# Attention with feature maps and two wide layers on one core: grouping the small matmuls and re-planning the order

## The chip, the cores and the metric

One core of a Trainium2 chip. The metric is the device time of one execution in microseconds (us). PE is the matmul engine, DVE the vector engine, ACT the scalar engine, POOL the general engine, SP the queue that issues the DMAs.

## What is computed

```python
def phi(x):                                   # x: 4 batches, 8 heads, 576 tokens, 64
    proj = np.einsum('bhsd,df->bhsf', x, w_phi)                   # 128 features
    proj = proj - np.max(np.abs(proj), axis=-1, keepdims=True)
    return np.concatenate([np.exp(proj), np.exp(-proj)], axis=-1)
q_p, k_p = (phi(q), phi(k))
kv = np.einsum('bhsf,bhsd->bhfd', k_p, v)
z = np.sum(k_p, axis=2)
num = np.einsum('bhsf,bhfd->bhsd', q_p, kv)
den = np.einsum('bhsf,bhf->bhs', q_p, z)[..., None] + 1e-06
x = num / den                                 # as 2304 tokens x 512
h = x @ w_in;  x = elu(h) @ w_out             # 512 -> 2048 -> 512
h = x @ w_in2; x = (h * cos(h)) @ w_out2      # 512 -> 2048 -> 512
```

## The kernel before, in words

The wide layers run as three passes of fp32r matmuls, high and low halves of both operands (`PASSES`). Layer 1 goes in two parts: the first 8 of 16 slices of d_ff over nine blocks of 256 tokens (part 0), then the other 8 over six blocks of 384 (part 1); layer 2 takes all 16 slices over six blocks of 384. For one block and one slice, `step` issues a group of 12 matmuls g1 (L636, into bank h), then the activation on ACT and DVE (L655, L658, L661 in layer 1; L670 to L682 in layer 2), the split into halves (L242 or L240 high, L694 low), and a group of 12 matmuls g2 (L644, into banks y). A block's own operand is split the same way (high half by ACT or DVE, low half by DVE, L595). Weights arrive packed; each of 128 pieces costs `convert_piece` and `split` three ACT instructions (L327, L330, L353), two on DVE (L334, L338) and two on POOL (L342, L356).

The attention is laid between the groups of part 0. `keys` takes the five key tiles of a batch: eight projections (L373), maximum and subtraction on DVE for each half of the heads ("odd" 0 and 1; L386, L389), two exponentials each on ACT (L423, L426), then the products with v (`times_v`, L431; for batch 0 also a sum over the tokens, L437). For the other batches the sum over the key tiles is made by additions of 1024 columns (L451), on POOL or DVE. `sums` turns the result (L488). `queries` and `results` do a tile of 128 queries: projections (L373), maximum and subtraction, four turns per half (L517), two exponentials per half (L520), 24 small matmuls per half (`product`, L535; 48 records where a matmul takes two), then L543, L546, L549 for the division, which writes the tile's part of the block's operand xy.

The order on every engine is made ahead of time. `body` lists tasks with an engine (or a choice of engines), a cost, a due time and what they wait for, and `plan` places them one by one: on the engine that can start first it takes, of the tasks that are ready, the one with the earliest due time. The due times come from the constants `BEGIN`, `BLOCK_A`, `LEAD`, `PACE` and so on. Until bank y1 is in use, `keep_busy` fills planned idle time of PE with matmuls on zeros ("spare", L749).

Of the kernel before, what the change touches and what calls it, by code (L numbers as in the profile page):

```python
# [13 lines left out]
ALU = mybir.AluOpType  # L14
# [34 lines left out]
SLACK = 1.0  # L49
# [36 lines left out]
class Task:  # L86


    def __init__(self, engine, cost, due, fn, writes=(), reads=(), after=(), latency=None, port=False):
# [3 lines left out]
        self.start = self.end = self.opens = None  # L93

# [27 lines left out]
def plan(tasks, opened):  # L122
# [29 lines left out]
    order, pooled = [], (0.0, 0.0)  # L152
    while len(order) < len(tasks):
        best = None
        for e, q in queues.items():
            cand = []
            for t in q:
                pl = place(t)
                if pl is not None:
                    slack = SLACK if t.engine == "SP" and pl[0] else 0.0  # L160
                    cand.append((max(t.ready, pl[0] + slack), t, pl[1]))
            if cand:
                first = max(free[e], min(c[0] for c in cand))
                c = min((c for c in cand if c[0] <= first), key=lambda c: c[1].due)
                if best is None or (first, c[1].choice[e]) < best[:2]:
                    best = (first, c[1].choice[e], e, c[1], c[2])
# [7 lines left out]
        for b, p in got:  # L174
            b.place = p
            held[p] = b
        t.start, t.end, t.cost = start, start + spent, spent
        if engine == "POOL":
            pooled = t.start, t.end
# [21 lines left out]
def mr_cost(n):  # L201

    return n * PE_COL + 0.013


def body(tc, qt, kt, vt, wphi, w1, w2, out):
# [54 lines left out]
    def buf(pool, tag, n, shape, dtype=F32):  # L261
        return Buf([(pool, f"{tag}{i}") for i in range(n)], shape, dtype)
# [102 lines left out]
    def shifted(x, due, r, ds, after, banks):  # L365
# [12 lines left out]
        task("PE", 1.04, due, project, pp, [x, c_w, *ds], after)  # L378
# [18 lines left out]
    def keys(b, due, pace, after=()):  # L397
# [4 lines left out]
        for t in range(5):  # L402
# [12 lines left out]
            if b == 0:  # L415
                shifted(kf, du - KFIRST, r, ds, (), ("a0", "a1", "h0", "h1"))
            else:
                shifted(kf, du, r, ds, (), AP)
            for odd in range(2):
                d, kv, e = ds[odd], kvs[odd], buf("at", "ek", NE, [P, 4, 2, NF])  # L420
# [7 lines left out]
                def times_v(kv=kv, e=e, v=v, t=t, r=r, odd=odd):  # L428
                    for i in range(4):
                        at, pair = 64 * (i % 2), i // 2  # L430
                        nc.tensor.matmul(  # L431
                            kv.tile[at:at + 64, pair * 256:pair * 256 + 256],
                            v.tile[0:r, 2 * i + odd], e.tile[0:r, i].rearrange("p s f -> p (s f)"),
                            start=(t == 0 and pair == 0), stop=(t == 4), skip_group_check=True,
                        )
                    for i in range(4 if zp else 0):
                        nc.tensor.matmul(  # L437
                            zp.tile[32 * i:32 * i + 32, 256 * odd:256 * odd + 256],
                            ones[0:r], e.tile[0:r, i].rearrange("p s f -> p (s f)"),
                            start=(t == 0 and odd == 0), stop=(t == 4), skip_group_check=True,  # L440
                        )

                a1 = task("ACT", cost(ACT_, 512), du, exp, [e], [d], d.ready)
                a2 = task("ACT", cost(ACT_, 512), du, exp_neg, [], [d, e], d.ready)
                if zp:
                    task("PE", 1.62, du, times_v, [kv, zp], [e, v], [a1, a2])
                    continue
                task("PE", 1.06, du, times_v, [kv], [e, v], [a1, a2])
                if t:
# [3 lines left out]
                    task("POOL", sums_of(1024), du, add, [totals[odd]], [e], [a1, a2])  # L453
# [42 lines left out]
    def queries(T, due, pace):  # L496
# [12 lines left out]
        for odd in range(2):  # L509
            results(T, odd, due + odd * pace / 2, parts, ds[odd], done)  # L510

    def results(T, odd, due, parts, d, done):
        e, m, tt, n = buf("at", "eq", NEQ, [P, 2, 4, P]), buf("at", "rd", 2, [P, P]), bank(*AQ), bank(*AQ)

        def turn():
            for h in range(4):
                nc.tensor.transpose(tt.tile[:, h * P:(h + 1) * P], d.tile[:, h], ident)  # L517

        def exp(neg):
            nc.scalar.activation(  # L520
                e.tile[:, neg], tt.tile.rearrange("p (h t) -> p h t", h=4), AF.Exp, scale=1.0 - 2 * neg
            )

        task("PE", 0.55, due, turn, [tt], [d, c_id], d.ready)
        a1 = task("ACT", cost(ACT_, 512), due, lambda: exp(0), [e], [tt])
        a2 = task("ACT", cost(ACT_, 512), due, lambda: exp(1), [], [tt, e])

        def product():
            for i, g in enumerate((2, 0, 1)):
                for b, lo, hi in parts:  # L530
                    k = kvz[b, odd].tile
                    for half in range(2):
                        for h in range(4):
                            at = 64 * (h % 2) + 32 * g
                            nc.tensor.matmul(  # L535
                                n.tile[32 * h:32 * h + 32, g * P + lo:g * P + hi],
                                k[:, half, h // 2, at:at + 32] if g < 2 else k[:, half, 2, 32 * h:32 * h + 32],
                                e.tile[:, half, h, lo:hi],
                                start=(i == 0 and half == 0 and lo == 0), stop=(half == 1), skip_group_check=True,
                            )  # L540

        def denominator():
            nc.scalar.activation(m.tile, n.tile[:, 2 * P:3 * P], AF.Identity, bias=eps)  # L543

        def inverse():
            nc.vector.reciprocal(m.tile, m.tile)  # L546

        def finish():
            nc.vector.tensor_tensor(  # L549
                out=xy[:, 2 * odd:2 * odd + 2, T * P:(T + 1) * P],  # L550
                in0=n.tile[:, 0:2 * P].rearrange("p (g t) -> p g t", g=2),
                in1=m.tile[:, None, :].to_broadcast([P, 2, P]), op=ALU.mult,
            )

        kz = [kvz[b, odd] for b, _, _ in parts]
        task("PE", 1.43 if len(parts) == 1 else 1.9, due, product, [n], [e, *kz], [a1, a2, *done])
        task("ACT", cost(ACT_, P), due, denominator, [m], [n])
        task("DVE", cost(RECIP, P), due, inverse, [m])
        xt[T] = xt.get(T, []) + [task("DVE", cost(DVE_, 256), due, finish, cells((2 * odd, 2 * odd + 1), T * P, P), [n, m])]


# [64 lines left out]
    def step(m, j, i, last, xs, ys, yp, hs, N, due, pace, late):  # L626
# [24 lines left out]
        in_line("g1", task("PE", 12 * mr_cost(N) + 0.05, d1, g1, [hp], [*wi, *x], line["g1"]))  # L651
# [161 lines left out]
```

## Time and profile before

| | us |
|---|---|
| three runs | 1006.4, 1008.87, 1006.4 (median 1006.4) |
| the profiled execution: span from first to last instruction | 1004.8 |
| PE busy in it | 986.5 (98%) |
| DVE, ACT, POOL busy | 730.0, 496.3, 241.9 |

The page gives no time for the profiled execution other than its span; the median of the runs is 1.6 us above it. Busy time of PE counts the spare matmuls. The times of instructions below are from the span's start.

### The profile page before, as it was taken

Reading aid. Unit: us, or ns where it says so; the run is one execution under the profiler, and the core shown is the slowest. Engines: PE = TensorE matmul, PEld = TensorE weight load, DVE = VectorE, ACT = ScalarE, POOL = GpSimd, SP = SyncE. Lnnn points to the kernel's source line nnn. Section 1 sums busy time; section 2 is a strip of 40 time slices with the busy share of each in tenths; the row PEclk is TensorE's granted clock in tenths of the full one; section 3 lists DMA queues with packets and bytes.
Section 4 is the critical chain, followed back from the end, with each engine's and each line's share of the span. In section 5 each row is a group of like instructions: output and inputs, shape, how many; then the busy total and the mean of one; then the engine's idle time right before and its main releaser. Section 6 shows DMA issues by size and latency. Waiting matters only on the chain.

```text
span 1004.8 us, 21194 instructions
## 1 busy us (share of the span) xinstructions
PE 986.5 (98%) x8404; PEld 943.2 (94%) x8404; DVE 730.0 (73%) x1434; ACT 496.3 (49%) x1192; POOL 241.9 (24%) x274
## 2 busy tenths in 40 slices
PE   9999999999999999999999999999999999999998
PEld 6797888998899999999999999999999999999998
DVE  6999788768677986997354699966666666666664
ACT  6987445545545875775232577532332232323322
POOL 2675303103101772774000276400000000000000
PEclk9999999999999999999999999999999999999999
DMA  6463031022102432441012143000000000000000
GB/s 197 163 201 102 7 107 54 30 78 59 39 13 96 151 124 87 160 158 36 8 32 74 64 137 113 29 33 1 1 32 1 1 33 1 33 1 1 32 1 32
DMA packets 46563, 63.30 MB, mean 63 GB/s; under 512 B 6400, under 2 KB 25472, under 8 KB 46464
## 3 DMA queue, kind: packets, MB, share of 16 engines
q1 hardware_dynamic: 46304, 61.88, 18.7%
q8 instruction: 66, 1.08, 0.5%
q14 instruction: 33, 0.27, 0.1%
q10 hardware_dynamic: 160, 0.07, 0.0%
HBM read 52.49 MB, written 9.44 MB: 62 GB/s over the span
## 4 chain that ended last, share of the span: by engine, by line
PE 81%; DVE 8%; POOL 3%; ACT 3%; issue 3%; DMA 1%; DVEq 0%; POOLq 0%; ACTq 0%
PE h L636 21%; PE y L644 20%; PE a L644 13%; PE a L636 13%; PE a L431 4%; PE a L535 4%; PE a L373 3%; POOL l L342 2%; DVE l L338 2%; POOL l L356 2%; PE a L517 1%; DVE l L334 1%; DVE u L694 1%; DVE u L595 1%; ACT l L327 1%
## 5 line engine op out<-in xcount | busy, mean ns | idle before, releaser
L636 PE MATMUL h<-u,h 128*128 128x256 f32 (+1 forms) x1152 | 254.6, 311 | 3.4 <-DVE u L661 3.4
L644 PE MATMUL y<-u,h 128*128 128x256 f32 (+1 forms) x1152 | 254.3, 311 | 1.0 <-DVE u L694 1.0
L636 PEld LDWEIGHTS h<-u,h 128*128 128x128 f32 x1152 | 191.9, 188 | 9.5 <-DVE u L661 4.2
L644 PEld LDWEIGHTS y<-u,h 128*128 128x128 f32 x1152 | 192.3, 188 | 4.6 <-issue 2.3
L644 PE MATMUL y<-u,l 128*128 128x256 f32 (+1 forms) x576 | 177.5, 308 | 0.0
L636 PE MATMUL h<-u,l 128*128 128x256 f32 (+1 forms) x576 | 177.5, 308 | 0.0
L342 POOL TENSOR_TENSOR l<-l,h 128x256 int32<-128x256 int32 x128 | 105.0, 825 | 247.4 <-ACT h L330 102.2
L636 PE MATMUL a<-u,h 128*128 128x384 f32 x576 | 147.3, 337 | 2.0 <-DVE u L595 1.0
L644 PE MATMUL a<-u,h 128*128 128x384 f32 x576 | 146.9, 336 | 0.9 <-DVE u L694 0.9
L694 DVE TENSOR_TENSOR u<-u,u 128x384 fp32r<-128x384 f32 (+1 forms) x216 | 123.1, 570 | 6.1 <-ACT u L240 0.7
L356 POOL TENSOR_TENSOR l<-l,h 128x256 fp32r<-128x256 f32 x128 | 106.7, 843 | 25.2 <-ACT h L353 24.5
L644 PEld LDWEIGHTS y<-u,l 128*128 128x128 f32 x576 | 108.4, 188 | 0.0
L636 PEld LDWEIGHTS h<-u,l 128*128 128x128 f32 x576 | 108.4, 188 | 0.0
L636 PEld LDWEIGHTS a<-u,h 128*128 128x128 f32 x576 | 103.9, 188 | 3.0 <-DVE u L595 1.7
L644 PEld LDWEIGHTS a<-u,h 128*128 128x128 f32 x576 | 104.0, 188 | 1.3 <-DVE u L694 1.3
L679 ACT ACTIVATE u<-u,pihalf 128x384 f32<-128x384 f32 x96 | 59.0, 616 | 90.8 <-DVE u L676 90.7
L636 PE MATMUL a<-u,l 128*128 128x384 f32 x288 | 96.8, 336 | 0.0
L644 PE MATMUL a<-u,l 128*128 128x384 f32 x288 | 96.8, 336 | 0.0
L655 ACT ACTIVATE u<-h 128x256 f32<-128x256 f32 (+1 forms) x96 | 39.1, 407 | 90.4 <-PE h L636 89.0
L242 DVE CAST u<-u 128x384 fp32r<-128x384 f32 (+1 forms) x157 | 61.4, 391 | 29.4 <-PE y L644 19.1
L338 DVE SCALAR_TENSOR_TENSOR l<-raw,l 128x256 uint32<-128x256 uint32 x128 | 72.2, 578 | 0.7
L661 DVE SCALAR_TENSOR_TENSOR u<-u,h 128x256 f32<-128x256 f32 (+1 forms) x96 | 42.6, 445 | 35.3 <-ACT u L658 34.9
(78 smaller groups left out, 1406.5 us busy)
## 6 DMA issues: line engine op xcount, KB each, us to landing
raw<-w SPq DMA_DIRECT2D x128, 256.0 KB, 3.0
qf<-qt SPq DMA_DIRECT2D x18, 256.0 KB, 2.9
part<-u SPq DMA_DIRECT2D x36, 128.0 KB, 1.8
u<-part SPq DMA_DIRECT2D x24, 192.0 KB, 2.5
out<-u SPq DMA_DIRECT2D x24, 192.0 KB, 1.9
kf<-kt SPq DMA_DIRECT2D x16, 256.0 KB, 3.7
vt<-vt SPq DMA_DIRECT2D x16, 256.0 KB, 4.3
kf<-kt SPq DMA_DIRECT2D x4, 128.0 KB, 2.7
```

The costliest lines, as they stand in the source:

```text
L242: engine.tensor_copy(dst, src)
L338: nc.vector.scalar_tensor_tensor(e, raw.tile[:, :, 1], 0x80000000, e, ALU.bitwise_and, ALU.bitwise_or)
L342: nc.gpsimd.tensor_tensor(e, e, r.tile, ALU.add)
L356: nc.gpsimd.tensor_sub(l.tile, f.tile, h.tile.bitcast(F32))
L431: nc.tensor.matmul(kv.tile[at:at + 64, pair * 256:pair * 256 + 256], v.tile[0:r, 2 * i + odd], e.tile[0:r, i].rearrange("p s f -> p (s f)" ...
L535: nc.tensor.matmul(n.tile[32 * h:32 * h + 32, g * P + lo:g * P + hi], k[:, half, h // 2, at:at + 32] if g < 2 else k[:, half, 2, 32 * h:32 ...
L636: nc.tensor.matmul(hp.tile[:, 0:N], columns(W[m, j, 0, kk * P // CH][a], kk), xs[kk][c].tile[:, 0:N], start=(kk == 0 and n == 0), stop=(kk ...
L644: nc.tensor.matmul(yp(dt), columns(W[m, j, 1, dt * P // CH][a], dt), (sh, sl)[c].tile[:, 0:N], start=(i == 0 and n == 0 and (late or dt % ...
L655: nc.scalar.activation(g.tile[:, 0:N], hp.tile[:, 0:N], AF.Relu, scale=-1.0)
L661: nc.vector.scalar_tensor_tensor(g.tile[:, 0:N], g.tile[:, 0:N], -1.0, hp.tile[:, 0:N], ALU.add, ALU.max)
L679: nc.scalar.activation(g.tile[:, 0:N], g.tile[:, 0:N], AF.Sin, bias=pihalf)
L694: nc.vector.tensor_sub(sl.tile[:, 0:N], g.tile[:, 0:N], sh.tile[:, 0:N].bitcast(F32))
```

## The change

The eight turns of a query tile become one task, its two products one task, and the products with v of a key tile (both halves, and both sums of batch 0) one task. The planner's choice on PE subtracts `STICK` from the due time of a task that is of the same kind as the last (g1 or g2 against all else), and adds `TURN` to the cost of a task of the other kind. Due times, some costs and buffer counts change (low halves of weights `NL` 6 to 4, query exponentials `NEQ` 3 to 4). What is computed stays the same.

```diff
-SLACK = 1.0
+SLACK = 0.97
+TURN, STICK = 0.1, 6.45
-BEGIN, BLOCK_A, BLOCK_B, BLOCK_C = 30.0, 42.0, 34.0, 68.0
-LEAD, PACE = 20.0, 28.0
-AHEAD = 3.0
-GATE = 2
-KLEAD, WSTART, WPACE = 25.0, 5.0, 7.0
-Q0, W2LATE, FILL = 15.0, 5.0, 0.7
-KFIRST, QFREE = 10.0, 5
-NL, W1LATE, NEQ, EARLY = 6, -20.0, 3, 180.0
+BEGIN, BLOCK_A, BLOCK_B, BLOCK_C = 31.56, 42.0, 34.0, 69.09
+LEAD, PACE = 25.76, 28.37
+AHEAD = 3.37
+GATE = 1
+KLEAD, WSTART, WPACE = 15.95, 5.0, 7.59
+Q0, W2LATE, FILL = 17.76, 6.61, 0.7
+KFIRST, QFREE = 3.52, 6
+NL, W1LATE, NEQ, EARLY = 4, -18.28, 4, 177.85
...
+        self.group = fn.__name__ in ("g1", "g2")
...
-                c = min((c for c in cand if c[0] <= first), key=lambda c: c[1].due)
+                c = min(
+                    (c for c in cand if c[0] <= first),
+                    key=lambda c: c[1].due - (STICK if e == "PE" and c[1].group == group else 0.0),
+                )
...
+        if engine == "PE":
+            spent += TURN if t.group != group else 0.0
+            group = t.group
...
-                task("PE", 1.06, du, times_v, [kv], [e, v], [a1, a2])
+            task("PE", 2.85 if zp else 1.76, du, times_v, [*kvs, zp] if zp else kvs, [*es, v], done)
...
-        task("PE", 0.55, due, turn, [tt], [d, c_id], d.ready)
+        task("PE", 0.87, due, turn, tts, [*ds, c_id], [t for d in ds for t in d.ready])
...
-        task("PE", 1.43 if len(parts) == 1 else 1.9, due, product, [n], [e, *kz], [a1, a2, *done])
+        task("PE", 2.65 if len(parts) == 1 else 3.5, due + pace / 2, product, ns, [*es, *kz], [*acts, *done])
```

The lines below that begin with L are those of the kernel's own file: L373 before is L382 after, L386 is L395, L389 is L398, L431 is L434, L437 is L441, L451 is L463, L595 is L619, L334 and L338 are L343 and L347, L661 is L685, L694 is L718, L242 is L251.

First place, PE, the second key tile of batch 0. Before (a: banks of the products with v, y: bank of the sums, ek: exponentials):

```order
L431 MATMUL a_33_190<-ek_36_204,vt_21_151 64x256 x4
L437 MATMUL y_34_191<-ek_36_204,ones 32x256 x4
L431 MATMUL a_42_229<-ek_37_208,vt_21_151 64x256 x4
L437 MATMUL y_34_191<-ek_37_208,ones 32x256 x4
L373 MATMUL a_66_316<-ww,kf_54_258 64x128
```

Now:

```order
L434 MATMUL a_39_211<-ek_38_206,vt_21_151 64x256 x4
L434 MATMUL a_40_212<-ek_42_231,vt_21_151 64x256 x4
L441 MATMUL y_41_213<-ek_38_206,ones 32x256 x4
L441 MATMUL y_41_213<-ek_42_231,ones 32x256 x4
L382 MATMUL h_59_295<-ww,kf_29_170 128x128
```

The two halves' matmuls of a kind now stand together.

Second place, DVE, the operand of the second block of part 0 (the four L595 whose input is xy are its low halves, and the first g1 of that block waits for the last of them). Before:

```order
L389 TENSOR_TENSOR d_289_1221<-a_287_1219,m_336_1454 128x512
L661 SCALAR_TENSOR_TENSOR u_337_1456<-u_337_1456,h_331_1429 128x256
L595 TENSOR_TENSOR u_346_1473<-xy,u_345_1472 128x256
L242 CAST u_352_1503<-u_337_1456 128x256
L595 TENSOR_TENSOR u_350_1485<-xy,u_349_1484 128x256
L694 TENSOR_TENSOR u_353_1504<-u_337_1456,u_352_1503 128x256
L595 TENSOR_TENSOR u_355_1507<-xy,u_354_1506 128x256
L334 TENSOR_SCALAR l_318_1355<-l_318_1355 128x256
L334 TENSOR_SCALAR l_327_1417<-l_327_1417 128x256
L595 TENSOR_TENSOR u_358_1519<-xy,u_357_1518 128x256
```

Now, the stretch that ends with the last of them:

```order
L685 SCALAR_TENSOR_TENSOR u_366_1558<-u_366_1558,h_349_1489 128x256
L619 TENSOR_TENSOR u_370_1571<-xy,u_369_1570 128x256
L251 CAST u_379_1597<-u_366_1558 128x256
L619 TENSOR_TENSOR u_372_1577<-xy,u_371_1576 128x256
L718 TENSOR_TENSOR u_380_1598<-u_366_1558,u_379_1597 128x256
L251 CAST u_381_1604<-xy 128x256
L395 TENSOR_REDUCE m_384_1610<-a_375_1585 128x4
L463 TENSOR_TENSOR ek_356_1523<-ek_356_1523,ek_374_1582 128x1024
L395 TENSOR_REDUCE m_386_1628<-a_376_1586 128x4
L398 TENSOR_TENSOR d_377_1587<-a_375_1585,m_384_1610 128x512
L398 TENSOR_TENSOR d_378_1588<-a_376_1586,m_386_1628 128x512
L619 TENSOR_TENSOR u_382_1605<-xy,u_381_1604 128x256
```

Key tiles of batch 1 now stand ahead of the last low half: up to and with that instruction DVE has 26 L386 and 26 L389 in its order where it had 20 and 20, one L451 where it had none, ten L242 where it had six, and 33 L334 where it had 34; all else is equal. On PE, three projections of key tiles and two groups of products with v (16 records each) have moved ahead of that block's first g1, and one g2 behind it.

Third place, DVE, the first weight pieces for part 1, which are converted while part 0 ends. Before:

```order
L694 TENSOR_TENSOR u_996_5117<-u_978_5058,u_995_5116 128x256
L338 SCALAR_TENSOR_TENSOR l_969_4994<-raw_968_4993,l_969_4994 128x256
L334 TENSOR_SCALAR l_972_4999<-l_972_4999 128x256
L334 TENSOR_SCALAR l_980_5061<-l_980_5061 128x256
L338 SCALAR_TENSOR_TENSOR l_972_4999<-raw_971_4998,l_972_4999 128x256
L338 SCALAR_TENSOR_TENSOR l_980_5061<-raw_979_5060,l_980_5061 128x256
L334 TENSOR_SCALAR l_991_5097<-l_991_5097 128x256
L338 SCALAR_TENSOR_TENSOR l_991_5097<-raw_990_5096,l_991_5097 128x256
L661 SCALAR_TENSOR_TENSOR u_1005_5169<-u_1005_5169,h_999_5129 128x256
```

Now:

```order
L347 SCALAR_TENSOR_TENSOR l_967_5024<-raw_966_5023,l_967_5024 128x256
L343 TENSOR_SCALAR l_973_5044<-l_973_5044 128x256
L343 TENSOR_SCALAR l_976_5049<-l_976_5049 128x256
L347 SCALAR_TENSOR_TENSOR l_973_5044<-raw_972_5043,l_973_5044 128x256
L347 SCALAR_TENSOR_TENSOR l_976_5049<-raw_975_5048,l_976_5049 128x256
L685 SCALAR_TENSOR_TENSOR u_992_5154<-u_992_5154,h_989_5123 128x256
L251 CAST u_997_5179<-u_992_5154 128x256
L718 TENSOR_TENSOR u_998_5180<-u_992_5154,u_997_5179 128x256
L685 SCALAR_TENSOR_TENSOR u_996_5177<-u_996_5177,h_991_5141 128x256
```

L661 empties a bank h that a later g1 waits for. Between two of them stood four L338 in two places of the last two blocks of part 0, and stand three at most now.

## Rows read from the trace of the kernel before

**Rows 1.** Busy time by stretch: us, engines' busy us (x instructions), PEclk, DMA share, GB/s
```profile
20.00:82.00 62.00, 57.72 (x821) 47.95 (x813) 59.09 (x120) 53.70 (x149) 45.28 (x59) 1.00 0.51 172
82.00:118.00 36.00, 35.99 (x335) 29.49 (x335) 31.60 (x61) 23.15 (x56) 17.73 (x13) 1.00 0.18 56
118.00:320.00 202.00, 200.40 (x3029) 180.34 (x3027) 150.92 (x287) 99.98 (x235) 23.20 (x9) 1.00 0.18 56
320.00:380.00 60.00, 57.26 (x477) 56.36 (x476) 55.48 (x117) 49.16 (x147) 44.61 (x55) 1.00 0.40 134
```

**Rows 2.** What PE waited for, whole span: us in total, times, longest
```profile
PE h L636 <- DVE u L661: 3.4, 4, 1.0
PE a L373 <- DMA kf<-kt: 1.3, 1, 1.3
PE a L517 <- DVE d L389: 1.3, 1, 1.3
...
PE a L535 <- issue: 1.1, 2, 0.6
PE a L636 <- DVE u L595: 1.0, 2, 0.9
...
PE a L636 <- DVE u L682: 1.0, 1, 1.0
PE a L644 <- DVE u L694: 0.9, 1, 0.9
```

**Rows 3.** The spare matmuls, from the groups: count, busy us, mean ns, idle before
```profile
L749 PE MATMUL spare<-idle 128*128 128x128 f32 x52 | 9.5, 330 | 1.1 <-DVE idle L744 1.1
```

**Rows 4.** Chain of waits, 0 to 92 us: start, us, what
```profile
11.78 1.01 PE a L431 x8
12.79 0.57 PE y L437 x8
```

**Rows 5.** Chain of waits, 60 to 130 us
```profile
81.25 0.61 DVE d L389
...
81.99 0.63 PE a L517 x4
...
90.00 1.09 PE a L373 x16
91.09 1.88 PE a L431 x16
92.97 1.62 PE h L636 x12
...
114.94 1.00 PE a L466 x16
...
119.66 1.42 PE h L636 x12
```

**Rows 6.** DVE in order of time, 79 to 92 us
```profile
83.37 0.28 DVE L242 CAST u<-u 128x256 fp32r<-128x256 f32 x1
83.57 0.41 DVE L595 TENSOR_TENSOR u<-xy,u 128x256 fp32r<-128x256 f32 x1
...
84.98 0.41 DVE L595 TENSOR_TENSOR u<-xy,u 128x256 fp32r<-128x256 f32 x1
...
85.99 1.27 DVE L386 TENSOR_REDUCE m<-a 128x4 f32<-128x512 f32 x2
87.19 1.27 DVE L389 TENSOR_TENSOR d<-a,m 128x512 f32<-128x512 f32 x2
```

**Rows 7.** PE in order of time, the first g1 of the second block
```profile
87.03 0.40 PE L636 MATMUL h<-u,h 128*128 128x256 f32 x2
```

**Rows 8.** DVE in order of time, 93 to 120 us, two of the 1024-column additions
```profile
96.32 2.16 DVE L451 TENSOR_TENSOR ek<-ek,ek 128x1024 f32<-128x1024 f32 x1
...
101.75 1.23 DVE L451 TENSOR_TENSOR ek<-ek,ek 128x1024 f32<-128x1024 f32 x1 [0.36 <-ACT ek L426]
```

**Rows 9.** The same addition on POOL, in order of time, 93 to 120 us
```profile
94.99 2.40 POOL L451 TENSOR_TENSOR ek<-ek,ek 128x1024 f32<-128x1024 f32 x1 [1.55 <-ACT ek L426]
```

**Rows 10.** All additions on POOL as a group, whole span, columns as in rows 3
```profile
L451 POOL TENSOR_TENSOR ek<-ek,ek 128x1024 f32<-128x1024 f32 (+1 forms) x12 | 33.4, 2786 | 128.7 <-ACT ek L426 128.7
```

**Rows 11.** Chain of waits, 325 to 380 us: three groups that began late
```profile
331.70 0.42 DVE u L661
332.16 1.68 PE h L636 x12
...
355.69 0.41 DVE u L661
356.15 1.70 PE h L636 x12
...
376.78 0.43 DVE u L661
377.25 1.70 PE h L636 x12
```

**Rows 12.** The product groups, from the chain over the whole span
```profile
71.88 1.52 PE a L535 x48
...
146.46 2.76 PE a L535 x96
...
199.22 1.45 PE a L535 x48
```

More of the change, by code (lines that the diff above doesn't have):

```diff
@@ L151, in plan @@
     free.update(START)
-    order, pooled = [], (0.0, 0.0)
+    order, pooled, group = [], (0.0, 0.0), None
     while len(order) < len(tasks):
@@ L176, in plan @@
             held[p] = b
+        if engine == "PE":
+            spent += TURN if t.group != group else 0.0
+            group = t.group
+        if engine == "POOL":
+            pooled = start, start + spent
         t.start, t.end, t.cost = start, start + spent, spent
-        if engine == "POOL":
-            pooled = t.start, t.end
         free[t.engine] = t.end
@@ L201, in mr_cost @@
 def mr_cost(n):
-    return n * PE_COL + 0.013
+    return n * PE_COL + (0.0115 if n < 384 else 0.013)
 def body(tc, qt, kt, vt, wphi, w1, w2, out):
@@ L376, in project @@
                     )
-        task("PE", 1.04, due, project, pp, [x, c_w, *ds], after)
+        task("PE", 1.02, due, project, pp, [x, c_w, *ds], after)
         for odd in range(2):
@@ L426, in exp_neg @@
                     nc.scalar.activation(e.tile[0:r, :, 1], d.tile[0:r], AF.Exp, scale=-1.0)
[L428 to L447, printed above, removed]
-                task("PE", 1.06, du, times_v, [kv], [e, v], [a1, a2])
+                done.append(task("ACT", cost(ACT_, 512), du, exp, [e], [d], d.ready))
+                done.append(task("ACT", cost(ACT_, 512), du, exp_neg, [], [d, e], d.ready))
+            task("PE", 2.85 if zp else 1.76, du, times_v, [*kvs, zp] if zp else kvs, [*es, v], done)
+            for odd in range(0 if zp else 2):
+                e, two = es[odd], done[2 * odd:2 * odd + 2]
                 if t:
@@ L451, in add @@
                         engine.tensor_add(total.tile[0:r], total.tile[0:r], e.tile[0:r])
-                    task("POOL", sums_of(1024), du, add, [totals[odd]], [e], [a1, a2])
+                    task("POOL", sums_of(1024), du, add, [totals[odd]], [e], two)
                 else:
@@ L508, in queries @@
         shifted(q, due, P, ds, () if T < QFREE else done, (*AQ, "h0", "h1") if T < 2 else AQ)
-        for odd in range(2):
[L510 to L522, printed above, removed]
-        task("PE", 0.55, due, turn, [tt], [d, c_id], d.ready)
-        a1 = task("ACT", cost(ACT_, 512), due, lambda: exp(0), [e], [tt])
-        a2 = task("ACT", cost(ACT_, 512), due, lambda: exp(1), [], [tt, e])
-        def product():
[L529 to L555, printed above, removed]
-        task("PE", 1.43 if len(parts) == 1 else 1.9, due, product, [n], [e, *kz], [a1, a2, *done])
-        task("ACT", cost(ACT_, P), due, denominator, [m], [n])
-        task("DVE", cost(RECIP, P), due, inverse, [m])
-        xt[T] = xt.get(T, []) + [task("DVE", cost(DVE_, 256), due, finish, cells((2 * odd, 2 * odd + 1), T * P, P), [n, m])]
```

69 lines of the change are left out of this document (67 added, 2 removed).

## The prediction

> **What bounds the kernel now.** I read the busy time by stretch first [rows 1]. From 82 us on PE is the bound: 35.99 of 36 us busy, then 200.40 of 202. Between 20 and 82 us it is not: DVE is busy for 59.09 of 62 us, and PE's 57.72 contain spare matmuls, which compute nothing. The groups put a number on those [rows 3]: 9.5 us in 52 records. So the start, in which keys are made and the first weights converted, is set by DVE; the long rest is set by the length of PE's stream plus a few waits. The list of PE's waits [rows 2] gives their size: the largest is 3.4 us in four waits of g1 for the activation L661. The chain of waits shows where three of these lie, in the last blocks of part 0: each time a L661 ends, and a group begins right after it [rows 11]. There DVE is converting weights for part 1 and is nearly full again, 55.48 of 60 us (last row of [rows 1]).
>
> The sum is made against the profiled execution, whose span is 1004.8 us; the median of the runs, 1006.4, is 1.6 us above it, and I add that again at the end. About 0.3%, 3 us, is what a measurement of this kernel can tell from no change: 1003.4 to 1009.4 counts as "same".
>
> **Merged groups.** Prices come from the steps of the chain. A product of 48 records takes 1.45 us, one of 96 takes 2.76 [rows 12]: two apart cost 2.90, so a merge saves 0.14. Products with v: 8 records 1.01 [rows 4], 16 records 1.88 [rows 5], again 0.14. The sums of batch 0: 0.57 for 8 [rows 4], and a group of the same shape (L466) 1.00 for 16 [rows 5], 0.14. The order before already has many pairs side by side: counted in it, runs of products fall from 18 to 13, runs with v from 26 to 20, runs of sums from 10 to 5. That is 16 merges of 0.14, or 2.3 us over the whole program; the turns are 4 records of 0.63 us on the chain when they wait [rows 5], and no row shows what two such runs save, so I take nothing, between 0 and 6 fewer runs at 0.14.
>
> **Like groups preferred.** A g1 between attention groups takes 1.62 us and one between its like 1.42 [rows 5]. The first has two changes of kind, so 0.1 each. Counted in the order, changes between g groups and others do not fall: they rise from 103 to 115. So the preference, as the planner uses it, costs 1.2 us on PE rather than saving anything. Merges and changes together leave PE's stream about 1 us shorter, but most of the merges lie in the start, where PE waits for DVE and a shorter stream gives nothing. Only what follows the start counts.
>
> **The second block's operand.** This is the term that decides. PE's first g1 of the second block starts at 87.03 [rows 7], after the fourth low half (L595) at 84.98 + 0.41 = 85.39 [rows 6]; the 1.64 us between are PE's own work. An operation on PE follows its DVE input by 0.13 us (81.25 + 0.61 = 81.86, then 81.99) [rows 5]. In the changed order DVE has more to do ahead of that low half: 6 L386 and 6 L389 at 0.60 each, since two L386 start 1.20 us before the next pair [rows 6], so 7.2 us; one addition of 1024 columns at 1.23 [rows 8]; four casts at 0.28 of row and about 0.05 of spacing, 1.3 [rows 6]; one L334 less, taken as long as a cast, 0.3. Together +9.4 us, and DVE has no slack but 62 − 59.09 = 2.9 us to take it in [rows 1]. The low half then ends at 85.39 + 9.4 = 94.8, and g1 starts at 94.9, 7.9 us later. The bound below is +5.0, where the order closes all of DVE's idle time; the one above comes with POOL.
>
> That last price has a row. The addition of 1024 columns takes 2.16 us on DVE while POOL runs the same from 94.99 to 97.39, and 1.23 us when alone [rows 8, 9]: 0.93 us lost of the 1.07 that the two overlap. All 12 additions on POOL took 2.79 us on average [rows 10], and before they all come after the early weight conversions; after the change four of 15 stand among these conversions, beside a full DVE. I take one such delay ahead of the operand, **+0.9**, between 0 and four of them, 3.7. The Trainium skill, "SBUF — State Buffer", section "SBUF: two separate sides", says that the port pair which DVE and GpSimd share is an exclusive lock, held for a whole instruction, so that the loser fully blocks. The trace agrees: DVE lost 0.93 of 1.07 us. By that rule an operation of DVE that is due just as POOL begins loses all of POOL's 2.79 us, four of them 11.2 us as an estimate, and the sum below would end near 1018 instead of 1008. The sum goes by the measured collision.
>
> Against the +7.9 stands the PE work that has moved ahead of that g1 and is then done: three projections of 1.09 and two groups with v of 1.88 [rows 5], 7.0 us, less one g2 of about 1.45 that moved behind: **−5.55**. Behind g1, counted in the order, there are 13 more changes of kind (+1.3), three fewer runs of products and one fewer with v (−0.55), and two more runs of the sums L466 (+0.3, at the same 0.14): **+1.0**. No other slack hides these, as PE is full there [rows 1].
>
> **The late waits.** Between two L661 stood four weight operations L338 in two places; each of these operations makes the next activation later, and three groups begin late [rows 11]. The change spreads them to three at most. The four waits are 3.4 us [rows 2], so three are about 2.6, and I take **−2.6**. Bounds: 0 if three L338 are enough to delay L661, and −5.3 if the fourth goes too, with the waits for L595 and L644 (1.0 and 0.9) [rows 2].
>
> **Moved without a price.** SP has the same number of rows in both orders and PE waits for a transfer once, 1.3 us at the start [rows 2]; the earlier key loads act only there. If the cover is gone (buffers `NL` from 6 to 4 hold back conversions), the first to be late is a low half of weights and then its g2, at about 1 us each as the waits of [rows 2] are. The end of the program keeps its rows.
>
> **Sum.** +7.9 + 0.9 − 5.55 + 1.0 − 2.6 = +1.65; the profile at about 1006.4, the runs at **1008.0**.
>
> **Rivals.** *POOL blocks DVE* (slower). Four POOL additions among the conversions each cost DVE 0.93 us, and the late waits stay. Then +7.9 + 3.7 − 5.55 + 1.0 = +7.05, 1013.5; with one collision +4.25, 1010.7; its middle 1012. For it: DVE is the bound exactly where the additions go [rows 1]. Against: not all meet a DVE operation with two inputs from memory. It decides from the point where the second block's first g1 starts later than 96 us.
>
> *The start is packed better* (faster). DVE does not idle before the operand, g1 starts at 92.0, and the waits for L661 and L644 go: +5.0 − 5.55 + 1.0 − 3.4 − 0.9 = −3.85, 1002.5. For it: the 2.9 us of idle DVE, and the 9.5 us of spare matmuls that show what PE could do [rows 3]. Against: DVE's idle time is in small pieces, each a wait for PE or ACT.
>
> *The preference does not do what it says.* It does not lower the changes of kind; that is in the sum at 1.3 us. If it did in fact act (12 changes fewer rather than more behind the start), the sum would be about 2.5 us lower, 1005.5, still "same".
>
> **How the numbers follow.** The forecast, with the preference either way, holds 0.38; the slower rival 0.34, since a full DVE leaves only its cover of 2.9 us; the faster rival 0.28, since the later waits are many and small and the order there is more even. Their times, 1008.0, 1012 and 1002.5, lie in same, slower and faster. The range goes to the slower rival's end, 1013.5, and 1 us below the faster one's time, 1001.5, since the waits for L595 [rows 2] could go too.
>
> **What would show it.** Right: the second block's first g1 at 94 to 96 us, no more spare time than 12 us plus about 2, and fewer L661 waits at 330 to 380. A g1 near 92 shows the packed start; one after 97, with additions on DVE or conversions of twice their length beside POOL, shows the slower rival. The forecast is wrong in kind if PE has new waits between 118 and 320 us, where it has 1.6 us idle now [rows 1].

## The result and the profile after

The changed kernel took 1019.0 us (median of four runs, 1016.1 to 1024.2), the kernel before 1006.4: a ratio of 1.0125, 95% interval 1.0095 to 1.0154. That is slower by more than the range allowed. The profiled execution is the one of 1019.5 us; its span is 1017.7 us, 12.9 more than before. Its mean granted clock, 0.991, is the lowest of the four (the others have 0.994 to 0.995), so what is said below of half clock holds for the execution that had most of it.

First the busy time by stretch of the changed kernel, in the columns of [rows 1]:

```profile
20.00:82.00 62.00, 58.53 (x841) 51.02 (x836) 59.85 (x123) 51.32 (x141) 41.74 (x55) 1.00 0.51 161
82.00:118.00 36.00, 31.74 (x274) 24.75 (x273) 35.70 (x58) 23.25 (x55) 20.19 (x16) 0.91 0.29 83
118.00:320.00 202.00, 198.45 (x2920) 178.51 (x2919) 142.87 (x277) 97.40 (x224) 29.73 (x13) 0.99 0.18 53
320.00:380.00 60.00, 59.87 (x574) 59.04 (x573) 44.33 (x105) 39.53 (x118) 26.52 (x33) 1.00 0.28 89
...
600.00:700.00 100.00, 96.59 (x542) 95.76 (x542) 79.08 (x153) 54.17 (x129) 35.65 (x44) 0.97 0.18 58
```

Against [rows 1], 320 to 380 us is better (PE 59.87 of 60, was 57.26). Between 82 and 118 us PE now idles for 4.3 us while DVE is full, and the granted clock, 1.00 in every stretch before, is 0.91 there, 0.99 up to 320 and 0.97 at 600 to 700. PE's waits, as in [rows 2], and the spare matmuls, as in [rows 3]:

```profile
PE a L382 <- issue: 4.1, 2, 3.6
PE a L660 <- DVE u L706: 3.4, 2, 2.1
PE a L554 <- issue: 2.7, 3, 1.2
...
PE a L668 <- DVE u L718: 1.5, 1, 1.5
```

```profile
L773 PE MATMUL spare<-idle 128*128 128x128 f32 x76 | 11.9, 301 | 1.1 <-DVE idle L768 1.1
```

The chain of waits from 85 us shows the first place, where [rows 5, 7] stood:

```profile
89.62 1.90 PE a L434 x16
91.52 3.57 issue
95.09 2.69 PE a L382 x16
97.78 2.86 PE h L660 x12
100.63 1.98 PE a L434 x16
102.61 1.61 PE h L660 x12
104.22 1.02 PE a L382 x16
```

PE idles 3.57 us, and then a projection takes 2.69 us instead of 1.09 and a g1 2.86 instead of 1.61. The windows show why: the clock is granted at half, the lower of its two levels (1.2 GHz), from 94 to about 101 us.

```profile
90.00:94.00 4.00, 1.50 (x14) 0.72 (x10) 4.00 (x4) 1.83 (x6) 1.91 (x1) 1.00 0.51 152
94.00:98.00 4.00, 2.91 (x17) 2.57 (x18) 4.00 (x9) 2.61 (x5) 1.67 (x2) 0.50 0.01 4
98.00:102.00 4.00, 4.00 (x24) 3.34 (x25) 4.00 (x5) 0.80 (x2) 4.00 (x3) 0.65 0.00 0
102.00:106.00 4.00, 4.00 (x41) 3.29 (x38) 4.00 (x9) 3.19 (x7) 3.06 (x4) 1.00 0.31 98
```

It falls twice more: near 272 us, where a g2 takes 2.86 us in the chain, and at 620 us, where layer 2 begins (chain of waits):

```profile
272.03 2.86 PE y L668 x12
...
622.47 4.17 PE a L660 x12
```

Where the 12.9 us are, by these rows. PE's idle time, stretch by stretch up to 700 us, is 19.7 us instead of 14.0: +5.6. The spare matmuls hold 2.4 us more. Half clock costs 1.6 + 1.25 us in the first place, about 1.6 at 272 (g2 +1.4, L478 +0.2) and about 3.0 at 620 (4.17 against 2.08, and 0.9 in the group ahead of it): 7.4. The remainder, −2.5 us, is PE's shorter stream.

Equal work on PE tells where they arise. At the 49th g1 both kernels have done the same groups on PE, but for the spare matmuls. PE in order of time, before and after:

```profile
323.81 0.40 PE L636 MATMUL h<-u,h 128*128 128x256 f32 x2
334.32 0.40 PE L660 MATMUL h<-u,h 128*128 128x256 f32 x2
```

The change is 10.5 us behind there. At the first g1 of layer 2 it is 9.0 behind (601.4 against 598.6, with three g2 of 2.08 us still to come), and at the end 12.9. So the start and the middle of part 0 lose 10.5 us, the late waits and the rest of layer 1 give 1.5 back, and the start of layer 2 loses 3.9.

DVE in order of time tells what PE waited for at 91.5 us, and POOL what held DVE:

```profile
89.59 2.47 DVE L251 CAST u<-xy 128x256 fp32r<-128x256 f32 x1
91.98 0.68 DVE L395 TENSOR_REDUCE m<-a 128x4 f32<-128x512 f32 x1
92.58 1.21 DVE L463 TENSOR_TENSOR ek<-ek,ek 128x1024 f32<-128x1024 f32 x1
93.72 0.68 DVE L395 TENSOR_REDUCE m<-a 128x4 f32<-128x512 f32 x1
94.32 1.27 DVE L398 TENSOR_TENSOR d<-a,m 128x512 f32<-128x512 f32 x2
95.51 0.41 DVE L619 TENSOR_TENSOR u<-xy,u 128x256 fp32r<-128x256 f32 x1
...
98.05 2.78 DVE L463 TENSOR_TENSOR ek<-ek,ek 128x1024 f32<-128x1024 f32 x1
...
110.59 3.69 DVE L463 TENSOR_TENSOR ek<-ek,ek 64x1024 f32<-64x1024 f32 x1 [0.30 <-ACT ek L454]
```

```profile
89.39 2.52 POOL L463 TENSOR_TENSOR ek<-ek,ek 128x1024 f32<-128x1024 f32 x1 [4.14 <-ACT ek L454]
...
97.21 2.54 POOL L463 TENSOR_TENSOR ek<-ek,ek 128x1024 f32<-128x1024 f32 x1
```

A cast that takes 0.28 us [rows 6] takes 2.47 while POOL adds from 89.39 to 91.91; two additions on DVE take 2.78 and 3.69 us against 1.21, each beside an addition on POOL. That is 6.2 us of DVE between 89 and 115. The projection at 95.09 begins when the first of the two L398 has emptied its bank; the block's own low half (L619) ends at 95.9, and its g1 stands behind that projection in PE's queue.

### The profile page after: what moved, and what is told of

Same layout as the page of the kernel before. It is cut to its first block, busy times and chain, and to the rows that moved or that the text cites. A ratio compares the mean times of both kernels' runs of the same rounds, so it can differ in the third digit from the quotient of the medians.

```text
span 1017.7 us, 21321 instructions
## 1 busy us (share of the span) xinstructions
PE 993.9 (98%) x8428; PEld 952.6 (94%) x8428; DVE 725.0 (71%) x1423; ACT 501.1 (49%) x1200; POOL 248.2 (24%) x277
## 4 chain that ended last, share of the span: by engine, by line
PE 86%; DVE 6%; issue 2%; ACT 2%; DMA 2%; POOL 1%; SPq 0%; DVEq 0%; POOLq 0%; ACTq 0%
PE y L668 23%; PE h L660 22%; PE a L668 14%; PE a L660 13%; PE a L554 4%; PE a L382 3%; PE a L434 3%; PE a L531 1%; DVE l L347 1%; DVE l L343 1%; DMA kf<-kt 1%; DVE u L718 1%; DMA raw<-w 1%; DVE u L685 0%; PE y L441 0%
## 5 line engine op out<-in xcount | busy, mean ns | idle before, releaser
L668 PE MATMUL a<-u,h 128*128 128x384 f32 x576 | 147.0, 336 | 1.5 <-DVE u L718 1.5
L718 DVE TENSOR_TENSOR u<-u,u 128x384 fp32r<-128x384 f32 (+1 forms) x216 | 124.4, 577 | 6.5 <-ACT u L249 1.5
L703 ACT ACTIVATE u<-u,pihalf 128x384 f32<-128x384 f32 x96 | 59.1, 616 | 87.8 <-DVE u L700 87.7
L251 DVE CAST u<-u 128x384 fp32r<-128x384 f32 (+1 forms) x149 | 54.2, 364 | 38.7 <-PE y L668 28.4
L347 DVE SCALAR_TENSOR_TENSOR l<-raw,l 128x256 uint32<-128x256 uint32 x128 | 73.4, 583 | 1.0
L685 DVE SCALAR_TENSOR_TENSOR u<-u,h 128x256 f32<-128x256 f32 (+1 forms) x96 | 42.8, 447 | 42.2 <-ACT u L682 42.1
```

Source lines behind the costliest of these rows:

```text
L251: engine.tensor_copy(dst, src)
L347: nc.vector.scalar_tensor_tensor(e, raw.tile[:, :, 1], 0x80000000, e, ALU.bitwise_and, ALU.bitwise_or)
L668: nc.tensor.matmul(yp(dt), columns(W[m, j, 1, dt * P // CH][a], dt), (sh, sl)[c].tile[:, 0:N], start=(i == 0 and n == 0 and (late or dt % ...
L685: nc.vector.scalar_tensor_tensor(g.tile[:, 0:N], g.tile[:, 0:N], -1.0, hp.tile[:, 0:N], ALU.add, ALU.max)
L703: nc.scalar.activation(g.tile[:, 0:N], g.tile[:, 0:N], AF.Sin, bias=pihalf)
L718: nc.vector.tensor_sub(sl.tile[:, 0:N], g.tile[:, 0:N], sh.tile[:, 0:N].bitcast(F32))
```

## The experiments

Theory A, formed on this profile: the loss lies in three stalls (DVE held by additions in the start, a short wait at 272 us, the late start of layer 2), each made longer by half clock. The rivals were that the time of these stalls only moves, and that one part of the change (merged groups, preference, due times) carries the loss. The changed kernel's plan was kept in most runs and single tasks moved in it; where constants changed, the order was planned anew. Each is compared with the kernel before on its own chip (1007 to 1009 us).

**Filling the idle time.** 

```diff
+        fill = {
+            nth("project", 13): (13, bank_of(nth("g1", 8)), True),
+            nth("g1", 124): (9, bank_of(nth("g2", 120)), True),
+            nth("g1", 125): (5, bank_of(nth("g2", 120)), True),
+        }
...
+                for _ in range(n):
+                    nc.tensor.matmul(tile_of(b)[:, 0:P], idle, idle, start=True, stop=True, skip_group_check=True)
```

> The changed kernel, with 13 spare matmuls on zeros ahead of the projection that waits at 91.5 us, 9 and 5 ahead of the two groups that wait at 616 and 621 us. Nothing else moves, so the waits themselves stay. Theory A (the idle PE is what brings the granted clock to half, and half clock costs about 2.95 us after the first wait and 2.8 after the last two): granted clock 1.00 at 94 to 102 and at 620 to 627, span 1012 (1017.7 less 5.7). Theory B (the clock falls for another reason, or the time lost is the waits alone): the clock still shows 0.50 in one of these stretches, span 1016 to 1019.

Ratio 1.0072 (1.0056 to 1.0088), span 1015.5. Windows of this run:

```profile
94.00:98.00 4.00, 3.33 (x32) 2.88 (x31) 4.00 (x9) 2.61 (x5) 1.47 (x2) 1.00 0.01 3
98.00:102.00 4.00, 4.00 (x34) 3.01 (x32) 4.00 (x4) 0.80 (x2) 4.00 (x3) 1.00 0.03 9
116.00:120.00 4.00, 3.78 (x23) 3.37 (x24) 2.67 (x8) 1.13 (x3) 1.84 (x2) 0.60 0.01 1
...
616.00:620.00 4.00, 3.96 (x29) 3.77 (x28) 3.53 (x8) 3.48 (x9) 2.27 (x3) 1.00 0.07 13
```

The clock is 1.00 in both filled places. In the start that shows idle PE as what brings it down: the change and three more runs that kept this wait of 3.6 us (`late_swap`, `after_late_conv`, `after_spread`) all have half clock behind it. At 620 us it shows less, because `defer_adds` (next) has two waits of 2.0 us there, unfilled, and no fall. Its windows:

```profile
612.00:616.00 4.00, 2.05 (x12) 1.73 (x10) 3.54 (x9) 3.97 (x10) 1.88 (x3) 1.00 0.35 115
616.00:620.00 4.00, 2.35 (x12) 2.03 (x12) 3.97 (x8) 3.14 (x9) 2.33 (x4) 1.00 0.45 134
620.00:624.00 4.00, 3.68 (x21) 3.68 (x22) 3.97 (x9) 3.00 (x8) 2.39 (x3) 1.00 0.54 177
```

Between the first and the ninth g1 of layer 2 `fill` gained 1.8 us on the change (2.8 expected). It also has no fall at 272 us, where nothing was filled; that gave 1.6 us between the 25th and the 41st g1, of which 1.1 were lost again before layer 2. In the start it gave nothing: the 17th g1 stands at 147.0 us, in the change at 146.8. PE, faster at 95 us, waited for an L398 at 114 to 116, and the clock fell behind that wait (waits of this run):

```profile
PE a L478 <- DVE d L398: 1.9, 1, 1.9
```

DVE is full until then, and PE cannot pass it.

**The additions behind the operand.** `first` is an addition that the plan has on DVE, `second` one that it has on POOL.

```diff
+        first, second = nth("DVE", "add", 0), nth("POOL", "add", 32)
+        last_low = nth("DVE", "low", 15)
...
+        second.engine = "DVE"
+        move(second, last_low)
+        move(first, last_low)
```

> The changed kernel with one move: the two additions of 1024 columns ahead of the second block's last low half, one on POOL and one on DVE, both run on DVE right behind that low half. Theory A (they held DVE for 2.2 us of blocking and 1.2 us of work, the bank of the next projection came free that much later, PE idled 3.6 us and the clock fell): projection at about 91.8, the second block's first g1 at about 92.9 instead of 97.7, no clock below 1.00 until 110 us, span 1013 to 1014. Theory B (the operand is late by the key tiles alone, and the additions only take the place of other waits): g1 after 95, span 1016 or more.

Ratio 1.0122 (1.0086 to 1.0158). The block's first g1 came at 93.2 us, the stall at 91.5 was gone, and the next wait was the largest:

```profile
PE a L478 <- DVE d L398: 2.8, 1, 2.8
```

Half clock came only behind that wait, from 113.9 us on. At the 17th g1 it was 0.9 us ahead of the change, about as much as DVE had gained (2.2 us of blocking less 1.2 of an addition more). So the operand's lateness is not the bound of the start; DVE's whole work until 116 us is. The times say less than the profile here: in the profiled execution, whose span is 1021.1 us, a group of 384 columns took 2.12 us instead of 2.08 from 623 us on, 185 groups, which makes 7.4 us. Two other executions took as long (1021.8 and 1023.3 us), the fourth 1015.3; that the same pace made the difference there is likely and not shown, as they left no trace. Without the 7.4 us the span would be 1013.7. Of these 4.0 us below the change 0.9 come from the start; most of the rest goes with the falls of the clock at 272 and 620 us, which this execution did not have.

**Four additions from POOL to DVE, in place.**

```diff
+        early = [t for t in order if t.flexible and t.fn.__name__ == "add" and t.engine == "POOL"][:4]
+        for t in early:
+            t.engine = "DVE"
```

> The changed kernel, with the first four additions of 1024 columns on DVE instead of POOL, at the same places in the order; nothing else moves. Theory A (POOL's addition holds DVE for as long as the two overlap): between 89 and 116 us the cast of 2.47 us on DVE takes 0.3, the additions of 2.78 and 3.69 us take 1.2; DVE gains 6.2 us there and does 4 x 1.2 = 4.8 us more, so the second block's first g1 is 1 to 2 us earlier and the span 1014 to 1017. Theory B (these DVE instructions are long for another reason, such as the transfers running then): they stay at 2.4 us or more, and the span grows by 4 us.

Ratio 1.0122 (1.0077 to 1.0166), span of the profiled execution 1014.3. DVE in order of time:

```profile
89.53 0.28 DVE L251 CAST u<-xy 128x256 fp32r<-128x256 f32 x1
89.73 1.21 DVE L463 TENSOR_TENSOR ek<-ek,ek 128x1024 f32<-128x1024 f32 x1
...
98.07 1.21 DVE L463 TENSOR_TENSOR ek<-ek,ek 128x1024 f32<-128x1024 f32 x1
```

The cast is back at 0.28 and the additions at 1.21: POOL's additions had held DVE. Now POOL is held instead:

```profile
109.08 3.52 POOL L351 TENSOR_TENSOR l<-l,h 128x256 int32<-128x256 int32 x1 [2.87 <-DVE l L347]
```

The block's first g1 came 1.1 us earlier and the 17th g1 1.8, about the 1.4 us net that DVE gained. So the collisions are a real but small part of the start; the stall stays (2.5 us) and half clock follows it. The span is 3.4 us below the change; the other 1.6 us are the fall at 272 us, which this execution did not have.

**The start of layer 2.** Seven runs moved work there. In the change ACT waits for POOL within weight conversions before it reaches the first activation (L694); the sums behind the last g2 (L635) end 0.24 us ahead of that activation, so either could hold it (DVE and ACT in order of time):

```profile
612.49 1.08 DVE L635 TENSOR_TENSOR xy<-a,u 128x384 f32<-128x384 f32 x2 [0.66 <-PE a L668]
613.16 0.41 ACT L362 CAST h<-l 128x256 fp32r<-128x256 f32 x1 [1.91 <-POOL l L351]
613.81 0.47 ACT L694 ACTIVATE u<-a 128x384 int32<-128x384 f32 x1
...
615.60 1.28 ACT L703 ACT_TABLE_LOAD   x1
616.89 0.61 ACT L703 ACTIVATE u<-u,pihalf 128x384 f32<-128x384 f32 x1
```

The load of a table on ACT ahead of L703, 1.28 us, lies in this chain too; the kernel before has the same one (603.90, 1.28 us), so it is not the difference. First the two g1 were put behind the last g2:

```diff
+        g2_last, g1_a, g1_b = nth("PE", "g2", 119), nth("PE", "g1", 121), nth("PE", "g1", 122)
+        move(g1_b, g2_last)
+        move(g1_a, g2_last)
```

> The changed kernel with one move: two g1 of the first block of layer 2 go behind the last two g2 of layer 1. Theory A (the first activation of layer 2 waits at 613.8 us for the buffer that the last sums of layer 1 hold, and these for the last g2): the waits at 618 and 622 us (3.4 us) and the half clock behind them (2.8 us) go, one wait of 0.7 us for the last g2's operand comes, span 1012. Theory B (weight conversions on ACT, DVE and POOL hold the activations there): the waits stay within 1 us, span 1016 to 1019.

Ratio 1.0096 (1.0079 to 1.0113); the waits for L706 fell only from 3.4 to 2.9 us. The last g2 alone does not set it. With this and the deferred additions:

> The two moves together. Theory A (independent stretches): their gains add, span about 1008, the runs about 1009 to 1010, near the kernel before. Theory B (what is gained in the start is lost again in later waits, as DVE has the same work to do): 1012 or more.

Ratio 1.0075 (1.0051 to 1.0098), span 1016.4: the gains did not add up to 1008. Then the conversions themselves were moved, on the change and on the variant with the old due times (`old_due` below), first all behind the fourth activation, then dealt out over eight steps (one cut of each edit):

```diff
+        late = [t for t in order[begin:end] if converts(t)]
...
+        at = order.index(nth("DVE", "times_h", 3)) + 1
+        order[at:at] = late
...
+            behind = nth("DVE", "low", 184 + i * 8 // len(moved))
+            least = place[t] = max(place[t], place[behind] + 0.5, least)
```

> The changed kernel with the start of layer 2 reordered: the last two g2 of layer 1 ahead of the second g1 of layer 2 (as in the run late_swap), and all weight-conversion steps on ACT, DVE, POOL and their loads that stand between there and the fourth activation of layer 2 moved behind that activation. Theory A (weight conversions hold the activations of layer 2): the waits at 616 to 622 us (3.4 us in the change, 2.9 in late_swap) fall below 1 us and no half clock follows, span 1011 to 1013. Theory B (the last g2 or the chain of the activation itself sets it, so conversions are not what is waited for): waits above 2 us there remain, span 1015 or more.

> The run old_due (merged groups and preference with the due times of before) with the same reordering at the start of layer 2: the last g2 of layer 1 ahead of the first g1 of layer 2, and the conversion steps behind the fourth activation. Theory A: the wait of 3.7 us at 610 us and the half clock behind it go, waits under 1 us, span 1001 to 1003, faster than before by 2 to 4 us. Theory B: a wait over 2 us remains there or comes up to 40 us later for a weight that was converted too late, span 1005 or more.

> The changed kernel with the start of layer 2 reordered: the last two g2 of layer 1 ahead of the second g1 of layer 2, and the weight-conversion steps from there on dealt out evenly behind the first eight steps of layer 2 (no step earlier than it stood). Theory A (the conversions hold the activations by standing in clumps ahead of one of them; the move of all behind the fourth only moved the wait to the fifth, 9 us): no wait over 2 us between 600 and 645 us, 4 us in all at most, span 1011 to 1014. Theory B (the conversions as a whole are too much work for these 35 us, however they are dealt): 4 us or more of waits and half clock there, 1016 or more.

> The run old_due with the same dealing, the last g2 of layer 1 ahead of the first g1 of layer 2. Theory A: waits at 600 to 645 us below 2 us in all instead of 3.7 us and half clock, span 1001 to 1004, not slower than before. Theory B: 4 us or more of waits there, 1007 or more.

None was better than the kernel it came from: ratios 1.0157, 1.0102, 1.0153 and 1.0093, with half-widths of 0.2 to 0.4%. The two on `old_due` are worse than it clear of these widths; the two on the change are not. Behind the fourth activation, the wait went to the fifth (PE in order of time, `after_late_conv`):

```profile
636.81 0.69 PE L668 MATMUL a<-u,h 128*128 128x384 f32 x1 [9.11 <-ACT u L249]
```

The first four activations no longer waited, so conversions do hold them. Dealt out, they made six smaller waits in `after_spread`, 5.9 us in all, and eight in `od_spread`, 6.6 us, none over 1.6 us. Theory B of these runs stands: the conversion work left at that point was too much for these 35 us in every order tried, and moving it only moved the wait. One more try, with the last g2 and the whole first activation ahead on the variant with the old due times, met the same wall at the second activation (a wait of 7.4 us for its L706; ratio 1.0083, 1.0055 to 1.0111):

> The merged groups and the preference with the due times of before, as in the run old_due, with one chain moved by hand: the last g2 of layer 1 ahead of the first g1 of layer 2, and behind it the two sums L635 on DVE and the whole first activation of layer 2 (L694, L697, L700, L703, L706) ahead of the weight conversions on ACT and DVE. Theory A (the first activation of layer 2 comes late, behind the last g2 and the conversions): the wait of 3.7 us at 610 us and the half clock behind it (about 2 us) go, a wait of at most 1.5 us for the second activation comes, span 1002 to 1004, runs about 3 us below old_due and not slower than before. Theory B (conversions are the bound there and only shift): span 1006 or more, with a wait for weights or for L718 in their place.

**The parts of the change.** The words behind # say which run has the line; they are not in the kernels.

```diff
-BEGIN, BLOCK_A, BLOCK_B, BLOCK_C = 31.56, 42.0, 34.0, 69.09
+BEGIN, BLOCK_A, BLOCK_B, BLOCK_C = 30.0, 42.0, 34.0, 68.0      # old_due, merge_only: and all others of before
-TURN, STICK = 0.1, 6.45
+TURN, STICK = 0.0, 0.0                                         # no_stick, merge_only
-AHEAD = 3.37
+AHEAD = 3.0                                                    # ahead3
```

> The merged groups and the preference of the change with the due times, buffer counts and GATE of before; the order is planned anew. In its order 25 L395 stand ahead of the second block's first g1 (26 in the change, 22 before), and the last g2 of layer 1 stands two g1 later than before. Theory A (the new due times and GATE cause the loss): 1005 to 1009, at or below before. Theory B (the merged groups cause it, as each asks for both halves at once and so waits longer): 1013 or more, with a PE stall over 2 us between 85 and 120 us.

> The small groups of before, with no preference, and the due times, buffer counts and GATE of the change. In its order 22 L386 stand ahead of the second block's first g1, and the last g2 of layer 1 as late as in the change. Theory A (due times): 1014 or more, with waits of about 3 us in all at the start of layer 2. Theory B (merged groups): 1005 to 1009 but for those waits, so 1007 to 1010, with no stall over 1.5 us between 85 and 120 us.

> The change without the preference for like groups and without its cost (both constants 0). 24 L395 stand ahead of the second block's first g1. Theory A (the preference puts key tiles ahead of the block's operand): the stall at 91 us is under 1.5 us, span 1011 to 1013. Theory B (preference without effect): stalls and clock as in the change, 1015 to 1019.

> The change with AHEAD back at 3.0 alone: the second group of a step is due 3.0 steps behind the first, not 3.37. The order is planned anew; at the start of layer 2 all but one of layer 1's last g2 stand ahead of the second g1 (in the change three stand behind the first), and 24 L395 stand ahead of the second block's first g1. Theory A (late g2 hold the banks that the activation of layer 2 needs): waits at 600 to 625 us under 1.5 us, no half clock there; with a shorter stall in the start, 1010 to 1013. Theory B (conversions hold it): waits of 3 us and half clock there, 1015 to 1019.

> The merged groups alone: due times, buffers and GATE of before, no preference and no cost for a change of kind; planned anew. Theory A (the groups themselves shorten PE's stream by about 2 us and bring no long stall): no stall over 1.5 us before 590 us, span to the start of layer 2 within 2 us of before, in all 1003 to 1008. Theory B (asking for both halves at once makes longer stalls): a stall over 2 us before 590 us, 1010 or more.

| ratio to before (95%) | due times of before | due times of the change |
|---|---|---|
| small groups, no preference | 1 | 1.0047 (1.0028 to 1.0066), `new_due` |
| merged groups, no preference | 1.0096 (1.0062 to 1.0130), `merge_only` | 1.0075 (1.0039 to 1.0112), `no_stick` |
| merged groups, preference | 1.0038 (1.0014 to 1.0063), `old_due` | 1.0125 (1.0095 to 1.0154), the change |

"Due times" here take in the buffer counts and `GATE`. The slower pace of 2.12 us a group is in some of these profiles too: by the same count it makes 2.9 us in `merge_only`, 3.1 in `ahead3`, 7.2 in `od_late_conv`, 1.1 in `both`, and nothing in the change, the kernel before and the others not named. How much of each median it makes is not known; `merge_only` without it (1016.8 us of span) still stands 9 us above `old_due` (1007.4).

`ahead3` stands at 1.0067 (1.0041 to 1.0094). By the expectations `old_due` is near theory A, `new_due` (1012 us) lies between its two, `merge_only` met theory B, and in `no_stick` the stall fell to 1.2 us, as theory A had it, but half clock followed even so. No cell is faster than before, and no single part carries the loss: grouping costs alone, the due times cost alone, and the preference helps beside the old due times (1.0096 to 1.0038) but not beside the new. Each plan has long stalls at other places. In `old_due` there is one, at the start of layer 2:

```profile
PE a L660 <- DVE u L706: 3.7, 1, 3.7
```

The last group of layer 1 ended where it did before (the first g1 of layer 2 at 596.0 us with one g2 of 2.08 still to come, 598.6 with none before), so up to there the groups and the preference cost nothing under these due times. In `ahead3` all but one of the last g2 stand ahead of the second g1 of layer 2 again; the waits there fell to 1.9 us (under 1.5 expected) and the clock stayed at 1.00, as expected; at 1014.8 us it is above the 1010 to 1013 expected.

## Why the prediction was wrong

The step that failed is the path in the start: the sum took it as bound by the second block's operand, and put the clock and the start of layer 2 at nothing. Its terms for the start, 7.9 + 0.9 − 5.55 + 1.0, make 4.25 us; at the 49th g1, with equal work done, the change was 10.5 us behind. Up to there PE idled 5.8 us more, ran spare matmuls for 2.4 us more and lost 4.4 us to half clock, with 2.1 us of shorter stream against it. The start of layer 2, which had no term at all, added 3.9 us.

**The second block's operand** was seen. Its low half ended at 95.9 us, where 94.8 plus the 0.9 for one collision were forecast, but that agrees by luck: the collision cost 2.2 us, and the rest of DVE's added work 8.3 instead of 9.4. g1 came at 97.7, not at 95.8. Three things were not in that step. First, the collision that I priced at 0.93 by [rows 8, 9] cost 2.2 us ahead of the operand and 6.2 until 115, more than the 3.7 us I gave as its bound: a collision costs what the two overlap, and I took one overlap's length as the price of all. The Trainium skill, "SBUF — State Buffer", section "SBUF: two separate sides", says of the pair of ports which the two share that whichever starts first has it for the whole instruction and the other fully blocks. The cast agrees with it: it started 0.2 us behind POOL's addition and ended 0.15 us behind its end. (The 1018 us that the rule's estimate gave is near the result by accident: the collisions held 6.2 us, not 11, and `flip4`, which took them away, moved the 17th g1 by 1.8.) Second, I followed the operand, but PE's queue had a projection ahead of g1, which waited for a bank behind the same DVE work; at half clock it took 1.6 us longer, and that is most of what lies between the operand and g1. Third, I took the stretch as bound by the operand; `defer_adds` and `fill` show that DVE is full until 116 us, so the work placed there counts as a whole, key tiles and additions of batch 1 alike.

**The −5.55 us of PE work moved ahead** held. g1 is 10.7 us later than before, and that is 5.55 of work, 3.6 of idle PE and 1.6 of half clock; 2.4 us more of spare matmuls are made up for by 2.0 of shorter stream and 0.4 less of other idle time.

**The clock** had no term. The trace of before shows 1.00 in every stretch, and I took it as fixed. New stalls, of 3.6 us in the start and of 3.4 us in layer 2 above all, were followed by half clock, 7.4 us of it in the profile; in the start `fill` shows that idle PE is its cause. Not all of that is net: without these three falls `fill` gained 1.8 us at 620, 1.6 at 272 and nothing in the start, where DVE would have held PE anyway.

**The late waits** came out as forecast: the three of [rows 11] are gone (−2.7 us). But I read the order only there. The start of layer 2 has no term in the sum, though the order showed three g2 of layer 1 moved behind the first g1 of layer 2; its waits were 3.4 us against 1.9, and half clock took 3.0. I had named buffers `NL` as a cover, with a low half of weights as the first to be late; late were the activations, behind conversions in ACT's queue.

**The merged groups** were worth more than priced. By the groups of the whole span the products take 0.7 us less (51.6 to 50.9), those with v 1.3 (40.3 to 39.0), the sums 1.0 (6.4 to 5.4), and the turns, for which I took nothing, 1.4 (20.5 to 19.1): −4.4, where I had −2.3. With the remainder of −2.5 above, changes of kind and the rest cost about 1.9, where I had counted 1.3 and 0.3. The price of a change rests on a reading that was off: the g1 of 1.42 us at 119.66 does not stand between its like, L488 follows it. And the g2 right behind L488, at 118.23, takes 1.43 us, so a change from L488 costs nothing in that trace.

Of the signs that the prediction named, the slower rival's was met (g1 after 97), and so was that of a forecast wrong in kind: PE idles 3.55 us between 118 and 320 us instead of 1.6. The slower rival had the right place, and `flip4` confirms its mechanism, for a part of the loss. Its doubt, that a collision needs a DVE operation with two inputs from memory, was too narrow: the cast, with one, lost 2.2 us. The rival stopped at 1013.5 because it too knew neither the clock nor layer 2. What remains open: why the merged groups alone make stalls of 1.2 and 2.3 us in the start of `merge_only`, which of the constants behind the due times does the harm, and how much of the net loss each fall of the clock has in the start, where DVE binds as well.

## What to carry to other kernels

Where an order is planned, read it at every place where an engine other than the bound one is full, not only where the trace of before shows waits: here each stage that was full on DVE or ACT gave back as a stall what was moved into it. Price a new PE stall of some microseconds with the half clock that may follow it; in this profile that took 7.4 us beside 5.6 us of added idle time. And a move that only exchanges places behind a full engine gained little here: the wait reappeared at the next thing that engine owed.

## What the runs showed of the hardware that was not expected

The clock does not follow the length of a wait alone. A wait of 3.6 us at 91.5 us was followed by half clock and one of 1.2 us at 125.8 was not, while two of 0.3 and 0.6 us with a product of 64 rows between them (268 to 271 us) were. In `flip4`, `fill` and `defer_adds` those at 268 to 271 us were not followed by it, with the same instructions around them; in `both` they were. Two waits of 2.0 us at 614 and 618 us in `defer_adds` were not, two of 2.1 and 1.4 us at 616 and 621 in the change were.

With a granted clock of 1.00, a group of 384 columns takes 2.08 us in most profiles and 2.12 us in long stretches of some (chain of waits, `defer_adds`):

```profile
701.15 2.12 PE h L660 x12
...
709.63 2.12 PE a L660 x12
```

The same group in the changed kernel:

```profile
703.60 2.08 PE h L660 x12
```

No instruction of these stretches differs between the two kernels; what sets this pace was not tried. It may be more of the scatter of the times than the clock is: of the change's four executions the longest, 1024.2 us, has the highest mean clock, 0.995, and two of `flip4`'s four are 7 us longer than the other two, at 0.995 and 0.997 against 0.993 and 0.996. That is not shown, as only profiled executions tell the pace.
